# Two-layer network behind an attention block: weights converted without GpSimd, a longer lag between the layers, the narrow block last

## The chip, the cores and the metric

The kernel runs on one core of one Trainium2 chip. The metric is device time in microseconds (us). Of the kernel before, three runs took 1065.77, 1066.15 and 1066.64 us; the median is 1066.15 us. Engines are named as the profile names them: PE (TensorE) with PEld (its weight loads), DVE (VectorE), ACT (ScalarE), POOL (GpSimd), SP (the queue that issues the DMAs).

## The reference, cut to what matters

12480 tokens of 128 channels pass an attention block with 32 inducing points, and then two layers of 2048 hidden units each.

```python
h = mab(I, x)            # 32 inducing rows look at all tokens (softmax over 12480)
a = mab(x, h)            # every token looks at the 32 rows
# first layer, float64 weights
g = s * relu(a @ w_in)**2 + b
y = g @ w_out
# second layer, float64 weights
h2 = y @ w2_in
g2 = where(h2 >= 1, h2, where(h2 <= -1, 0, (h2 + 1)**2 / 4))
out = g2 @ w2_out
```

The four weight matrices arrive as float64, two 32-bit words to a number. [...]

## The kernel before

**Blocks and steps.** The tokens are cut into 25 blocks (`NB`): 24 of 512 tokens and one of 192. The narrow one is block 0 (`tokens`, L86). The 2048 hidden units of a layer are 16 chunks of 128; a step takes two chunks of one block, so a block has 8 steps (`SPB`) and a layer 200. In step t the first layer works on its step t (`in1`, relu, square, split, `out1`) and the second layer on step t minus `LAG` (`in2`, clip, square, `g2`, split, `out2`). `LAG` is 13. A matmul with float32 operands is issued in one piece, and split products (an fp32r high part and an fp32r rest) take three matmuls in place of one.

**Three parts of the program.** In the ramp, a planner (class `Plan`, L102) gives every operation an engine and a start from fixed costs and dependencies, and emits all operations in the order of their planned starts; `JOBS` (L67) is the order in which it is asked. The ramp holds the pass over x (loads, transposes, scores, running maximum and sum, weighted sums) that ends with `hT`, the transposed attention rows; the conversion of the weights; the product of `hT` with `w_in` (`h_w`), which replaces the first matmul of the layer's own weights; and the first 13 steps of the first layer, whose `out1_whole` (L697) multiplies in float32, since the split weights aren't there yet. Then a plain loop (L1025) issues step after step in the order of `ORDER` (L72). The last steps are planned again, in the order of `TJOBS` (L78).

**Conversion.** The weights are 16 pieces of 128x512 numbers (`pieces`, four each of `w_in`, `w_out`, and then `w2_in` and `w2_out` in turn). `convert` (L398) squares the upper word on ACT (L409), makes a mask from it on DVE (L423), shifts and joins the exponent and mantissa bits on DVE (L426, L430), masks the power of two on DVE (L434), scales the lower word on POOL (L415), multiplies (L437) and adds (L442) on POOL. For the second layer's weights a high part (L444) and a rest (L447) follow, the rest by a subtraction in DVE or POOL (L449). `split_out` (L470) does the same for half of `w_out`.

**PSUM.** The tag `h1` has one buffer of two banks, `h2` has two; the ramp's products `pw`, the scores of the first groups and the steps' `in1` take them in turn, and `took` (L826) gives the planner the release that an operation has to wait for. `y1` and `y2` have one bank each.

Of the kernel before, what the change touches and what calls it, by code (L numbers as in the profile page):

```python
# [34 lines left out]
LAG = 13  # L35
# [25 lines left out]
ENG = {"mask": ("DVE",), "sq": ("ACT", "Pool"), "lo": ("Pool",), "mul": ("Pool",), "add": ("Pool",),  # L61
       "hi": ("ACT", "Pool", "DVE"), "rest": ("DVE", "Pool")}
# [39 lines left out]
class Plan:  # L102
# [3 lines left out]
    HOP = 0.2  # L106
    SAME = {"DVE": 0.13, "ACT": 0.15}
# [4 lines left out]
    def find(self, eng, dur, deps, at):  # L112
        t = at
        for d in deps:
            if d is not None:
                t = max(t, d[1] + (self.SAME.get(eng, 0.0) if eng == d[2] else self.HOP))
        line = self.lines.setdefault(eng, [])
        for i, (a, b) in enumerate(line):
            if b <= t:
                continue  # L120
            if a - t >= dur:
                return t, i
            t = max(t, b)
# [1024 lines left out]
```

## Time and profile before

| | |
|---|---|
| median of three runs | 1066.15 us |
| the profiled execution | 1066.77 us, its span 1065.0 us |
| PE busy | 1020.1 us, 96% of the span |
| DVE busy | 834.6 us, 78% |
| ACT busy | 769.1 us, 72% |
| POOL busy | 667.9 us, 63% |
| chain that ended last | PE 88%, DVE 7% |
| mean granted PE clock | 0.977 of full speed |

The table is an average over parts that have different limits. The page's 40 slices show this: PE reads 9 tenths or more from the sixth slice to the last but one, and 7, 7, 7, 4, 8 in the first five, in which the clock row reads 7 to 9 tenths too. The rows below therefore go by stage: up to `hT`, from `hT` to the second layer's first matmul, the settling of both layers, the long even part, and the end.

### The profile page before, as it was taken

What the parts mean: (1) busy time and instruction counts of PE and PEld (TensorE: products, weight loads), DVE (VectorE), ACT (ScalarE), POOL (GpSimd) and SP (SyncE); (2) the same over time, 40 slices, a digit from 0 to 9 for tenths busy, and PEclk for the clock granted to TensorE, in tenths of its full rate; (3) what the DMA queues carried; (4) which work ended last, traced back from release to release, by engine and by line L of the source; (5) the groups of instructions that cost most, each with busy time, mean ns of one, the idle gap of its engine ahead of it and who ended that gap; (6) DMA issues with size and microseconds to landing.
All of it is one profiled execution on the core that took longest, in us unless ns stands there. A gap on an engine that the chain in (4) does not pass through costs nothing.

```text
span 1065.0 us, 11873 instructions
## 1 busy us (share of the span) xinstructions
PE 1020.1 (96%) x4285; PEld 748.9 (70%) x4285; DVE 834.6 (78%) x821; ACT 769.1 (72%) x807; POOL 667.9 (63%) x656
## 2 busy tenths in 40 slices
PE   7774899999999999999999999999999999999997
PEld 5553577777777777777777777777777777777775
DVE  5889768777788777788778788777788778777775
ACT  5425477777777777777777777777777777777754
POOL 3666776656657656567566567565675665656565
PEclk9777899999999999999999999999999999999999
DMA  8522001100001000001000002000011000000001
GB/s 282 198 60 59 1 4 30 20 11 1 11 11 39 10 11 1 11 10 40 10 10 11 1 11 50 0 11 10 1 24 37 0 10 10 1 10 10 10 1 20
DMA packets 65466, 28.25 MB, mean 27 GB/s; under 512 B 54016, under 2 KB 58240, under 8 KB 65408
## 3 DMA queue, kind: packets, MB, share of 16 engines
q1 hardware_dynamic: 65408, 27.49, 10.6%
q8 instruction: 34, 0.56, 0.2%
q14 instruction: 24, 0.20, 0.1%
HBM read 14.80 MB, written 6.39 MB: 20 GB/s over the span
## 4 chain that ended last, share of the span: by engine, by line
PE 88%; DVE 7%; ACT 1%; issue 1%; POOL 1%; DVEq 0%; ACTq 0%; POOLq 0%
PE y L692 15%; PE y L679 9%; PE y L678 8%; PE y L680 8%; PE h L729 8%; PE h L728 8%; PE h L727 8%; PE h L637 8%; PE y L695 4%; PE y L694 4%; PE y L693 4%; DVE g L655 1%; DVE cva_out L426 1%; PE s L572 0%; DVE cva_out L430 0%
## 5 line engine op out<-in xcount | busy, mean ns | idle before, releaser
L734 DVE TENSOR_SCALAR cl<-h 128x1024 f32<-128x1024 f32 (+2 forms) x202 | 238.7, 1184 | 121.0 <-PE h L729 121.0
L201 POOL TENSOR_SCALAR hi<-g 128x512 fp32r<-128x512 f32 x187 | 131.5, 703 | 309.6 <-PE y L695 306.3
L648 ACT ACTIVATE g<-h 128x1024 f32<-128x1024 f32 (+1 forms) x200 | 200.8, 1004 | 158.3 <-PE h L637 155.9
L756 DVE TENSOR_TENSOR lo<-oo,hi 128x1024 fp32r<-128x1024 f32 (+1 forms) x188 | 238.4, 1268 | 69.1 <-ACT hi L197 54.8
L738 ACT ACTIVATE cl<-cl,mhalf 128x1024 f32<-128x1024 f32 (+2 forms) x202 | 226.0, 1121 | 67.5 <-DVE cl L734 67.5
L663 POOL TENSOR_TENSOR lo<-g,hi 128x512 fp32r<-128x512 f32 x187 | 242.3, 1296 | 15.6
L743 DVE SCALAR_TENSOR_TENSOR oo<-h,cl 128x1024 f32<-128x1024 f32 (+2 forms) x202 | 237.2, 1176 | 8.6 <-ACT cl L738 5.1
L653 ACT ACTIVATE g<-g 128x1024 f32<-128x1024 f32 (+1 forms) x195 | 205.0, 1051 | 5.4
L692 PE MATMUL y<-g,wo_w 128*128 128x512 f32 x374 | 191.0, 591 | 0.0
L727 PE MATMUL h<-y1h,wi_hi 128*128 128x512 f32 (+1 forms) x400 | 155.8, 389 | 3.3 <-DVE oo L743 3.3
L678 PE MATMUL y<-hi,wo_hi 128*128 128x512 f32 (+1 forms) x400 | 157.5, 394 | 0.6 <-ACT hi L197 0.6
L729 PE MATMUL h<-y1l,wi_hi 128*128 128x512 f32 (+1 forms) x400 | 156.7, 392 | 0.0
L680 PE MATMUL y<-hi,wo_lo 128*128 128x512 f32 (+1 forms) x400 | 156.7, 392 | 0.0
L728 PE MATMUL h<-y1h,wi_lo 128*128 128x512 f32 (+1 forms) x400 | 156.0, 390 | 0.0
L679 PE MATMUL y<-lo,wo_hi 128*128 128x512 f32 (+1 forms) x386 | 152.6, 395 | 0.9 <-DVE lo L756 0.8
L693 PE MATMUL y<-hi,wo_hi 128*128 128x512 f32 x187 | 148.3, 793 | 0.0
L637 PE MATMUL h<-qt,hw 128*128 128x512 f32 (+1 forms) x400 | 126.3, 399 | 2.4 <-ACT g L648 1.3
L197 ACT CAST hi<-oo 128x1024 fp32r<-128x1024 f32 (+2 forms) x106 | 105.2, 996 | 3.7 <-PE y L680 1.9
L201 POOL TENSOR_SCALAR hi<-oo 128x1024 fp32r<-128x1024 f32 (+1 forms) x96 | 99.3, 1034 | 0.5 <-DVE oo L743 0.5
L678 PEld LDWEIGHTS y<-hi,wo_hi 128*128 128x128 f32 x400 | 75.5, 189 | 22.7 <-POOL lo L663 4.2
L637 PEld LDWEIGHTS h<-qt,hw 128*128 128x128 f32 x400 | 74.6, 189 | 23.6 <-ACT g L648 3.3
L727 PEld LDWEIGHTS h<-y1h,wi_hi 128*128 128x128 f32 x400 | 75.4, 188 | 21.1 <-issue 2.1
(148 smaller groups left out, 1188.6 us busy)
## 6 DMA issues: line engine op xcount, KB each, us to landing
xc<-in_x_dram SPq DMA_DIRECT2D x24, 256.0 KB, 5.6
qin<-se SPq DMA_DIRECT2D x96, 64.0 KB, 2.0
out_dram<-o SPq DMA_DIRECT2D x96, 64.0 KB, 2.2
raw_in<-in_moe_w_in_dram SPq DMA_DIRECT2D x8, 512.0 KB, 5.3
raw_out<-in_moe_w_out_dram SPq DMA_DIRECT2D x8, 512.0 KB, 5.1
xc<-in_x_dram SPq DMA_DIRECT2D x1, 96.0 KB, 1.9
out_dram<-o SPq DMA_DIRECT2D x4, 24.0 KB, 2.7
ind_sb<-in_inducing_dram SPq DMA_DIRECT2D x1, 16.0 KB, 5.1
```

The costliest lines, as they stand in the source:

```text
L637: nc.tensor.matmul(p[:, j, :tb(bl)], hw[f // 4][:, (f % 4) * 128:(f % 4 + 1) * 128], qt[bl], start=True, stop=True)
L663: engine[eng].tensor_sub(lo1[t], g1[t][:, 1:], hi1[t].bitcast(F32))
L678: nc.tensor.matmul(p, whi[:, f, :], hi[:, j, :], start=first, stop=False)
L679: nc.tensor.matmul(p, whi[:, f, :], lo[:, j, :], start=False, stop=False)
L680: nc.tensor.matmul(p, wlo[:, f, :], hi[:, j, :], start=False, stop=last)
L692: nc.tensor.matmul(p, wo_w[:, f0, :], g[:, 0, :], start=(f0 == 0), stop=False)
L727: nc.tensor.matmul(p[:, j, :tb(bl)], wi2_hi[:, fs], y1h[bl], start=True, stop=False)
L728: nc.tensor.matmul(p[:, j, :tb(bl)], wi2_lo[:, fs], y1h[bl], start=False, stop=False)
L729: nc.tensor.matmul(p[:, j, :tb(bl)], wi2_hi[:, fs], y1l[bl], start=False, stop=True)
L734: nc.vector.tensor_scalar(cl[t][:, part(js)], h2[t][:, part(js), :tb(t // SPB)], -1.0, 1.0, op0=ALU.max, op1=ALU.min)
L743: nc.vector.scalar_tensor_tensor(oo[t][:, part(js)], h2[t][:, part(js), :tb(t // SPB)], -1.0, cl[t][:, part(js)], op0=ALU.max, op1=ALU.add)
L756: engine[eng].tensor_sub(lo2[t][:, part(js)], oo[t][:, part(js)], hi2[t][:, part(js)].bitcast(F32))
```

## The change

**Conversion.** ACT takes the absolute value of the upper word, DVE raises it to a smallest value and shifts it (two one-operand operations in place), joins sign and exponent (`c_a`), masks the power of two (`c_p`) and does scaling and multiplication of the lower word in one two-operand operation (`c_mul`). For `w_in` and `w_out` a sum on DVE or POOL follows (`c_add`). For the second layer's weights there is no sum on DVE or POOL: the high part is a copy of the upper sum `cva` on ACT or DVE, and the rest is made on PE, which adds `cva`, minus the high part and the lower word through three matmuls with identity matrices into a PSUM bank of the tag `h2`; ACT or DVE copies the bank out (`c_lo`).

**Plan.** The planner's costs are new, and it has a line "port": an operation on POOL or one on DVE that is marked `DVE+` takes the port for its whole length, so that it never plans the two side by side. Waits for a PSUM buffer also keep the order in which the buffers are taken (`took`). Squares and relus of the ramp's steps may go to ACT or DVE.

**Lag and blocks.** `LAG` is 18, so the ramp holds 18 steps of the first layer, and the last 18 steps hold the second layer alone. The narrow block is block 24, the last; the ramp's steps are all 512 wide. `JOBS` puts weight pieces ahead of x. `YB` is 3. The last steps' jobs are written by `last_jobs`, with every high part on ACT and every rest on POOL.

```diff
-LAG = 13
+LAG = 18
-YB = 2
+YB = 3
-ENG = {"mask": ("DVE",), "sq": ("ACT", "Pool"), "lo": ("Pool",), "mul": ("Pool",), "add": ("Pool",),
-       "hi": ("ACT", "Pool", "DVE"), "rest": ("DVE", "Pool")}
+TS, TT = 0.42, 0.69
+ENG = {"add": (("DVE+", TT), ("Pool", 1.27)), "hi": (("ACT", 0.59), ("DVE+", TS)), "rest": (("DVE+", TT), ("Pool", 1.27)),
+       "lo": (("ACT", 0.59), ("DVE", 0.65))}
...
-x0 c0 i t0 x1 c1 it x2 c2 t1 s0 w0 s1 c3 x3 x4 t2 s2 t3 c4 w1 s3 w2 t4 c5 s4 x5 c6 t5 x6 w3 t6 w4 s5
+c0 i c1 it x0 c2 t0 s0 c3 x1 x2 t1 t2 s1 c4 w0 x3 s2 x4 t3 w1 x5 w2 x6 s3 t4 w3 b4 t5 s4 w4 s5 t6 s6 w5 f z h0 h1 c5
...
 def tokens(bl):
-    if bl:
-        return TP, KB, TB, TB0 + (bl - 1) * TB
-    return TP0, KB0, TB0, 0
+    if bl < NB - 1:
+        return TP, KB, TB, bl * TB
+    return TPL, KBL, TBL, bl * TB
...
     def find(self, eng, dur, deps, at):
+        name = eng.rstrip("+")
+        lines = [self.lines.setdefault(k, []) for k in [name] + (["port"] if eng in ("DVE+", "Pool") else [])]
...
-        def c_t1():
-            nc.vector.scalar_tensor_tensor(new("cva", U32), T["raw", n][:, :, 1], 3, T["cvs", n].bitcast(U32),
-                                           op0=ALU.logical_shift_left, op1=ALU.bitwise_and)
+        def c_abs():
+            nc.scalar.activation(new("cvs", F32), T["raw", n][:, :, 1].bitcast(F32), AF.Abs)
+        def c_top():
+            nc.vector.tensor_scalar_max(T["cvs", n], T["cvs", n], TINY)
+        def c_shift():
+            v = T["cvs", n].bitcast(U32)
+            nc.vector.tensor_scalar(v, v, 3, 0x3FFFFFF8, op0=ALU.logical_shift_left, op1=ALU.bitwise_and)
...
-        def c_mul(eng):
-            engine[eng].tensor_mul(T["cvl", n], T["cvl", n], T["cvs", n])
+        def c_mul():
+            nc.vector.scalar_tensor_tensor(new("cvl", F32 if name in ("in", "out") else F32R), T["raw", n][:, :, 0], 2.0 ** -52, T["cvs", n],
+                                           op0=ALU.mult, op1=ALU.mult)
...
-        def c_rest(eng):
-            hi, lo = (w[:, sl] for w in wparts[name])
-            engine[eng].tensor_sub(lo, T["w", n], hi.bitcast(F32))
+        def c_sum():
+            ps = T["cw", n] = mbank(f"cw{n}")[:, 0, :]
+            nc.tensor.matmul(ps, ident, T["cva", n].bitcast(F32), start=True, stop=False)
+            nc.tensor.matmul(ps, minus_r, wparts[name][0][:, sl], start=False, stop=False)
+            nc.tensor.matmul(ps, ident_r, T["cvl", n], start=False, stop=True)
+        def c_lo(eng):
+            copy(eng, wparts[name][1][:, sl], T.pop(("cw", n)))
...
-        p = mbank(f"h1_{t}") if t < LAG and t % 3 else bank(f"h1_{t}")
+        p = mbank(f"h1_{t}") if t < LAG and t % 2 else bank(f"h1_{t}")
...
-TH = "APPAAAAAAAPAA"
-TL = "PPPPPPPPPDPPD"
+TH = "A"
+TL = "P"
```

**How it moves instructions: one weight piece.** On DVE before, the second piece (`cvs_in_236`, `cva_in_250`) is four instructions, and the pass over x follows:

```order
L423 TENSOR_SCALAR cvs_in_236<-cvs_in_236 128x512
L426 SCALAR_TENSOR_TENSOR cva_in_250<-raw_in_193,cvs_in_236 128x512
L430 SCALAR_TENSOR_TENSOR cva_in_250<-raw_in_193,cva_in_250 128x512
L434 TENSOR_SCALAR cvs_in_236<-cva_in_250 128x512
L293 TENSOR_REDUCE mx_293<-psc_230 128x1
L296 TENSOR_TENSOR m_292<-mx_293,m_202 128x1
L298 TENSOR_SCALAR nm_296<-m_292 128x1
L346 COPY hsum<-ph_275 128x128
```

On POOL before, the same piece (`cvl_in_238`) and the loads of the next two:

```order
L415 TENSOR_SCALAR cvl_in_238<-raw_in_193 128x512
L437 TENSOR_TENSOR cvl_in_238<-cvl_in_238,cvs_in_236 128x512
L442 TENSOR_TENSOR win<-cvl_in_238,cva_in_250 128x512
L415 TENSOR_SCALAR cvl_in_321<-raw_in_243 128x512
L415 TENSOR_SCALAR cvl_in_331<-raw_in_266 128x512
```

On DVE now, the second piece is `cvs_in_164`, `cva_in_183`, `cvl_in_199`:

```order
L440 TENSOR_SCALAR cvs_in_164<-cvs_in_164 128x512
L444 TENSOR_SCALAR cvs_in_164<-cvs_in_164 128x512
L447 SCALAR_TENSOR_TENSOR cva_in_183<-raw_in_147,cvs_in_164 128x512
L451 TENSOR_SCALAR cvs_in_164<-cva_in_183 128x512
L454 SCALAR_TENSOR_TENSOR cvl_in_199<-raw_in_147,cvs_in_164 128x512
L460 TENSOR_TENSOR win<-cvl_in_199,cva_in_183 128x512
L509 COPY iT<-pi 128x32
```

Six instructions stand on DVE where four stood, and the three on POOL are gone.

**The second layer's beginning.** On PE before, behind the first layer's step 12 (`g_12` is its squared product, `y_1` its output) and one more `in1`, the second layer begins with `h_0`, 192 columns wide:

```order
L702 MATMUL y_1_1013<-g_10_1024,wo_w 128x512
L702 MATMUL y_1_1013<-g_10_1024,wo_s 128x512
L702 MATMUL y_1_1013<-g_11_1042,wo_w 128x512
L702 MATMUL y_1_1013<-g_11_1042,wo_s 128x512
L702 MATMUL y_1_1013<-g_12_1055,wo_w 128x512
L702 MATMUL y_1_1013<-g_12_1055,wo_s 128x512
L637 MATMUL h_13_1077<-qt_976,hw_827 128x512
L637 MATMUL h_13_1077<-qt_976,hw_907 128x512
L727 MATMUL h_0_1080<-y1h_1037,wi_hi 128x192
L728 MATMUL h_0_1080<-y1h_1037,wi_lo 128x192
```

On PE now, the last `in1` of this stretch, the float32 products of steps 16 and 17 and the sum of the last weight piece (`cw_1160`) stand ahead of the second layer's `h_0`:

```order
L657 MATMUL h_19_1134<-qt_1023,hw_806 128x512
L657 MATMUL h_19_1134<-qt_1023,hw_829 128x512
L726 MATMUL y_2_1142<-g_16_1088,wo_w 128x512
L726 MATMUL y_2_1142<-g_16_1088,wo_s 128x512
L726 MATMUL y_2_1142<-g_17_1125,wo_w 128x512
L726 MATMUL y_2_1142<-g_17_1125,wo_s 128x512
L468 MATMUL cw_1160<-cva_out_1149,ident 128x512
L469 MATMUL cw_1160<-wo_hi,minus_r 128x512
L470 MATMUL cw_1160<-cvl_out_1155,ident_r 128x512
L751 MATMUL h_0_1167<-y1h_991,wi_hi 128x512
L752 MATMUL h_0_1167<-y1h_991,wi_lo 128x512
L753 MATMUL h_0_1167<-y1l_998,wi_hi 128x512
```

The second layer's first matmul has moved from behind step 13's `in1` to behind step 19's, the float32 products reach to step 17 (`g_17`) and not to step 12, a sum of three matmuls stands ahead, and `h_0` is 512 wide.

**The end.** On PE before, the second layer's last `in2` (`h_199`) stands behind the `out2` of step 195 (`hi_195`; its rest lies in a buffer named `g_195`), 512 wide:

```order
L678 MATMUL y_24_8623<-hi_195_8638,wo_hi 128x512
L679 MATMUL y_24_8623<-g_195_8652,wo_hi 128x512
L680 MATMUL y_24_8623<-hi_195_8638,wo_lo 128x512
L727 MATMUL h_199_8677<-y1h_8452,wi_hi 128x512
L728 MATMUL h_199_8677<-y1h_8452,wi_lo 128x512
L729 MATMUL h_199_8677<-y1l_8461,wi_hi 128x512
```

On PE now, the `in2` of step 198 (`h_198`) stands behind the `out2` of step 192 (`hi_192`, `lo_192`):

```order
L702 MATMUL y_24_8627<-hi_192_8574,wo_hi 128x192
L703 MATMUL y_24_8627<-lo_192_8598,wo_hi 128x192
L704 MATMUL y_24_8627<-hi_192_8574,wo_lo 128x192
L751 MATMUL h_198_8640<-y1h_8333,wi_hi 128x192
L752 MATMUL h_198_8640<-y1h_8333,wi_lo 128x192
L753 MATMUL h_198_8640<-y1l_8335,wi_hi 128x192
```

The last eight steps, 192 to 199, are 192 wide and not 512, and `in2` runs six steps ahead of `out2` there, not four.

## Rows read from the trace of the kernel before

**Rows 1.** Windows by stage: length; busy PE, PEld, DVE, ACT, POOL (count); clock; DMA; GB/s

```profile
0.00:62.85 62.85, 49.28 (x420) 35.75 (x420) 43.15 (x86) 29.85 (x64) 33.32 (x39) 0.82 0.62 211
62.85:116.25 53.40, 34.93 (x122) 21.86 (x121) 50.98 (x67) 20.44 (x32) 38.35 (x32) 0.80 0.18 50
116.25:163.44 47.19, 43.94 (x213) 32.85 (x212) 32.21 (x45) 38.03 (x44) 33.71 (x34) 0.96 0.02 3
163.44:1006.98 843.54, 843.54 (x3340) 621.90 (x3339) 667.40 (x586) 650.69 (x635) 525.78 (x530) 1.00 0.07 13
1006.98:1059.20 52.22, 48.43 (x198) 36.52 (x196) 40.15 (x40) 30.13 (x33) 36.70 (x22) 1.00 0.07 11
1059.20:1065.00 5.80, 0.00 (x0) 0.00 (x0) 0.72 (x1) 0.00 (x0) 0.00 (x0) 0.93 0.30 45
```

**Rows 2.** Timeline of DVE: the first conversion; hT. Start, length, engine, line, operation, [idle before]

```profile
8.72 0.43 DVE L423 TENSOR_SCALAR cvs_in<-cvs_in 128x512 f32<-128x512 f32 x1 [6.47 <-ACT cvs_in L409]
...
62.56 0.29 DVE L546 COPY hT<-pht 128x128 f32<-128x128 f32 x1 [0.41 <-PE pht L521]
```

**Rows 3.** Timeline of PE: the longest wait; the second layer begins

```profile
90.29 5.07 PE L702 MATMUL y<-g,wo_s 128*128 128x192 f32 x16 [6.65 <-DVE g L655]
...
116.25 0.25 PE L727 MATMUL h<-y1h,wi_hi 128*128 128x192 f32 x1
```

**Rows 4.** Timeline of PE, one full step

```profile
163.44 0.63 PE L637 MATMUL h<-qt,hw 128*128 128x512 f32 x2
...
163.91 0.39 PE L727 MATMUL h<-y1h,wi_hi 128*128 128x512 f32 x1
...
165.30 0.40 PE L678 MATMUL y<-hi,wo_hi 128*128 128x512 f32 x1
...
166.71 1.02 PE L692 MATMUL y<-g,wo_w 128*128 128x512 f32 x2
...
168.26 0.63 PE L637 MATMUL h<-qt,hw 128*128 128x512 f32 x2
```

**Rows 5.** Timeline of PE, a narrow step of the second layer

```profile
139.31 0.25 PE L727 MATMUL h<-y1h,wi_hi 128*128 128x192 f32 x1
...
139.96 0.27 PE L678 MATMUL y<-hi,wo_hi 128*128 128x192 f32 x1
```

**Rows 6.** Timeline of PE near the end: a wait for VectorE

```profile
1033.60 0.47 PE L727 MATMUL h<-y1h,wi_hi 128*128 128x512 f32 x1 [1.73 <-DVE oo L743]
```

**Rows 7.** Timeline of DVE near the end: 1024 columns, both operands in SBUF

```profile
1052.28 1.23 DVE L756 TENSOR_TENSOR lo<-oo,hi 128x1024 fp32r<-128x1024 f32 x1 [0.19 <-ACT hi L197]
```

**Rows 8.** Windows of DVE before hT: lines L423, L426, L430, L434, L199 in turn

```profile
0.00:62.85 62.85, 8.23 (x10) 0.82 0.62 211
...
0.00:62.85 62.85, 8.45 (x9) 0.82 0.62 211
...
0.00:62.85 62.85, 7.88 (x9) 0.82 0.62 211
...
0.00:62.85 62.85, 3.48 (x9) 0.82 0.62 211
...
0.00:62.85 62.85, 0.40 (x1) 0.82 0.62 211
```

**Rows 9.** Timeline of DVE, one piece alone, then one beside GpSimd

```profile
17.01 0.43 DVE L423 TENSOR_SCALAR cvs_in<-cvs_in 128x512 f32<-128x512 f32 x1 [4.78 <-ACT cvs_in L409]
17.47 0.69 DVE L426 SCALAR_TENSOR_TENSOR cva_in<-raw_in,cvs_in 128x512 uint32<-128x512 uint32 x1
18.19 0.69 DVE L430 SCALAR_TENSOR_TENSOR cva_in<-raw_in,cva_in 128x512 uint32<-128x512 uint32 x1
...
38.22 1.66 DVE L426 SCALAR_TENSOR_TENSOR cva_out<-raw_out,cvs_out 128x512 uint32<-128x512 uint32 x1
```

**Rows 10.** Timeline of POOL at the same place

```profile
37.98 1.35 POOL L442 TENSOR_TENSOR wo_w<-cvl_out,cva_out 128x512 f32<-128x512 f32 x1
```

**Rows 11.** Window in which PE waited

```profile
85.00:90.00 5.00, 0.00 (x0) 0.00 (x0) 4.93 (x5) 1.12 (x2) 4.37 (x3) 0.50 0.42 103
```

More of the change, by code (lines that the diff above doesn't have):

```diff
@@ L1 @@
+import bisect
 import math
@@ L102 @@
 class Plan:
-    HOP = 0.2
-    SAME = {"DVE": 0.13, "ACT": 0.15}
+    HOP = {"PE": 0.25}
+    SAME = {"DVE": 0.04, "ACT": 0.05, "Pool": 0.05}
     def __init__(self):
@@ L192, in moe_attn_kernel, with took @@
     add, best = plan.add, plan.best
+    left = {"h1": [None], "h2": [None, None]}
+    last = {"h1": 0.0, "h2": 0.0}
+    def took(tag, dur, fn, *deps):
+        op = add("PE", dur, fn, *deps, left[tag][-1 if tag == "h1" else -2], at=last[tag])
+        last[tag] = op[0]
+        return op
     engine = {"ACT": nc.scalar, "DVE": nc.vector, "Pool": nc.gpsimd}
@@ L444, in c_hi @@
         def c_hi(eng):
-            copy(eng, wparts[name][0][:, sl], T["w", n])
-        def c_rest(eng):
-            hi, lo = (w[:, sl] for w in wparts[name])
-            engine[eng].tensor_sub(lo, T["w", n], hi.bitcast(F32))
-        free = P.get(("c_end", n - CVB))
-        raw = P["raw", n]
-        cost = {"mask": {"DVE": 0.34}, "sq": {"ACT": 0.52, "Pool": 1.45}, "lo": {"ACT": 0.52, "Pool": 0.59}, "mul": {"Pool": 1.23, "DVE": 0.6},
-                "add": {"Pool": 1.23, "DVE": 0.6}, "hi": {"ACT": 0.52, "Pool": 0.59, "DVE": 0.34},
-                "rest": {"Pool": 1.23, "DVE": 0.6}}
@@ L466, in convert @@
-        if name in wparts and name != "out":
-            hi = best(one_of["hi"], c_hi, ad)
-            P["c_end", n] = best(one_of["rest"], c_rest, hi)
+            copy(eng, wparts[name][0][:, sl], T["cva", n].bitcast(F32))
+        def c_sum():
[3 more added lines that the diff above has]
+            nc.tensor.matmul(ps, ident_r, T["cvl", n], start=False, stop=True)
@@ new lines, in c_lo @@
+        def c_lo(eng):
+            copy(eng, wparts[name][1][:, sl], T.pop(("cw", n)))
+        t = add("ACT", 0.68, c_abs, P["raw", n], P.get(("c_end", n - CVB)), at=at)
+        t = add("DVE+", TS, c_top, t)
+        t = add("DVE+", TS, c_shift, t)
+        a = P["c_a", n] = add("DVE+", TT, c_a, t)
+        t = add("DVE+", TS, c_p, a)
+        t = P["c_mul", n] = add("DVE+", TT, c_mul, t)
+        if name in ("in", "out"):
+            P["c_add", n] = P["c_end", n] = best(ENG["add"], c_add, t, bias=CB)
+        else:
+            hi = best(ENG["hi"], c_hi, a)
+            t = took("h2", 1.33, c_sum, hi, t, P["hT"])
+            P["c_end", n] = best(ENG["lo"], c_lo, t)
+            left["h2"].append(P["c_end", n])
@@ L958, in plan_step @@
         if name == "in1":
-            stage(name, u, "PE", 0.41, in1, p("qt", bl), free("relu1", u, 1, "h1"), p("in1", u - 1))
+            stage(name, u, "PE", pe(GW, bl), in1, p("qt", bl), free("relu1", u, 1, "h1"), p("in1", u - 1))
         elif name == "relu1":
@@ L975, in plan_step @@
         elif name == "in2":
-            stage(name, u, "PE", 1.22, in2, p("y1", bl), wchunk("in2", u), free("g2", u, 2, "h2"), p("in2", u - 1))
+            stage(name, u, "PE", pe(6, bl), in2, p("y1", bl), wchunk("in2", u), free("g2", u, 2, "h2"), p("in2", u - 1))
         elif name == "clip2":
@@ L988, in plan_step @@
         elif name == "out2":
-            stage(name, u, "PE", 1.22, out2, p("lo2", u), wchunk("out2", u), p("out2", u - 1), p("store", u // SPB - 1))
+            stage(name, u, "PE", pe(6, bl), out2, p("lo2", u), wchunk("out2", u), p("out2", u - 1), p("store", u // SPB - 1))
     def both_steps(t):
```

256 lines of the change are left out of this document (124 added, 132 removed).

## The prediction

> **What bounds the kernel now.** I read the windows by stage first, then the chain of waits on the page, then the timelines of PE and DVE. The windows cut the run into five parts [rows 1]. From 163.44 to 1006.98 us PE is busy for all of 843.54 us at clock 1.00, with DVE at 79% and ACT at 77%: there PE alone sets the time, and only PE work taken out of this part, or moved ahead of it, is worth anything. From hT (62.85 us, [rows 2]) to the second layer's first matmul (116.25 us, [rows 3]) PE is busy for 34.93 of 53.40 us at a mean clock of 0.80, and DVE for 50.98: there DVE binds. Up to hT neither is full (PE 49.28, DVE 43.15 of 62.85). So the ramp, which DVE paces, has free PE time, and the even part has none.
>
> A full step is in1 0.47, in2 1.39, out2 1.41, out1 1.55 us, 4.82 in all [rows 4]. A fp32r matmul of 512 columns takes 0.47/2 = 0.235 there, so the float32 one in out1 takes 1.55 - 3 x 0.23 = 0.86. A narrow step's in2 takes 0.65 [rows 5]; I take 0.66 for its out2, and 0.87 for its in1 and out1 together (five matmuls at 0.11, and 0.86 x 192/512 = 0.32).
>
> **PE work behind the second layer's first matmul (call its start S).** Before, S is 116.25, and steps 14 to 199 of in1 and 13 to 199 of out1 are still to come, with the whole second layer: 186 x 0.47 + 187 x 1.55 + 192 x 2.80 + 8 x 1.31 + 24 blocks' scores at 0.25 = 87.4 + 289.9 + 537.6 + 10.5 + 6.0 = 931.4 us. (The 0.25: the even part's 843.54 us are 174 steps at 4.82, 838.7, and five groups of four blocks' scores, so 0.97 a group.) The rest of the span is 1065.0 - 116.25 = 948.8, so 17.4 us are no matmul at full clock: 5.8 behind the last one [rows 1], about 5 of waits among the last steps (the longest 1.73, [rows 6]), and 6.4 while the layers settle up to 163.44.
>
> Now, step 19's in1 and step 17's out1 stand ahead of S. Left are 172 full in1 (80.8), 174 full out1 (269.7), 8 narrow steps of the first layer (7.0), the second layer as before (537.6 + 10.5) and 20 blocks' scores (5.0): 910.6. That is 20.8 less. Two edits share it: five steps of lag, and a narrow block that no longer uses up eight of the ramp's steps. Waits behind S: 5.5 behind the last matmul (transpose and store are narrower, the DMA's own delay stays), 5.5 at the end, and 3 while the layers settle, since in2 of step 2 must wait for the clip chain of step 0: 14.0. The bounds of this term are 9 and 20: at the lower end no settling and little waiting among narrow steps, at the upper end POOL, which now makes every rest, and DVE, which has 1.23 us for a full-width two-operand operation [rows 7] and three such each step, pace the eight mixed steps and the last ten full ones. So the span is S + 910.6 + 14.0 = S + 924.6.
>
> **S, first part: hT.** The five conversion lines take 8.23 + 8.45 + 7.88 + 3.48 + 0.40 = 28.4 us of DVE before hT [rows 8], so the pass over x takes 43.15 - 28.4 = 14.7. A piece alone shows what an operation costs from start to start: 0.46 with one tensor operand, 0.72 with two [rows 9]. Beside POOL it costs more: the one at 38.22 takes 1.66 instead of 0.69, while POOL's sum holds from 37.98 to 39.33 [rows 9, 10]. Now six pieces with six operations each (3 x 0.46 + 3 x 0.72 = 3.54) are 21.2, two with five are 5.6, and two operations of the ninth 0.9: 27.7. DVE therefore works 42.4 us before hT, as before; the change is that it may wait less. Before, it waited 19.7 us: 6.47 of it for the first piece, which came behind four loads of x [rows 2], and more for later pieces, which ran behind x too. Now the pieces' loads go ahead of x. I take a start at 5.5 (no sooner than 5, no later than the 8.72 of before) and 5 of waits in the last chain of small operations through PE, ACT and DVE: hT at 53. Its bounds are 48 and 63, the latter if x, now behind 0.5 to 1 MB of weights, ends the pass as late as before.
>
> **S, second part: from hT to S.** On DVE stand: the rest of eight pieces, 8 x 2.82 - 0.9 = 21.7; 16 squares 1024 wide, by the nearest row 1.23 and a gap, 1.26 each [rows 7] = 20.2; four products with the attention rows, 2.9; the softmax of the first block and of the first group, an estimated 6.8 (six full-width operations at 0.72 and small ones); three turns, two rests and one copy at 0.72, 4.3. Sum 55.9. This is more than the 50.98 of before, with five more steps done in it. Waits: 5 in the first 8 us, where the first softmax goes back and forth between PE, DVE and ACT; 3 for relus later; 2 for the few operations left on POOL, which can each cost a DVE operation about 1 us. So 66 us, and S = 53 + 66 = 119. Bounds are 57 (nearly no waits) and 80 (below). ACT was busy for 20.44 of 53.40 there [rows 1]; even twice that fits into 66. PE has in the same 66 us: 20 in1 (9.4), 18 out1 in float32 at 2 x 0.86 (31.0), eight sums at 0.86 + 0.47 (10.6), four products (3.4), scores and small ones (1.8): 56.2 at full clock. It fits, but with 10 us to spare, and this is the step I trust least.
>
> **Sum.** 119 + 924.6 = 1043.6 us of span. The profiled execution's time was 1066.77 with a span of 1065.0, 1.8 more, and the median of the runs is 0.6 below that execution, so 1043.6 + 1.2 = **1044.8 us**, against 1066.15.
>
> **Where a page and the rows are weighed.** In the window from 85 to 90 us PE has no work and its clock reads 0.50, the lower level of 1.2 GHz [rows 11]; its wait there lasts 6.65 us [rows 3]. In the even part the clock is 1.00 [rows 1]. The Trainium skill ("TensorE: Matmul & The Clock Gate", part 1) says that the lower clock is the state at rest and that sustained work releases the upper one. By that rule, and the trace agrees, a ramp in which PE works for 56 of 66 us would run mostly at the upper level, and the sum above stands; a ramp with holes in it would not, and that is the second and the last case below.
>
> **The rivals.**
> (a) *PE becomes the bound of the ramp.* If the clock between hT and S stays at the mean of before, 0.80 [rows 1], PE needs 56.2 / 0.80 = 70 us, and starts in earnest some 8 us behind hT: S = 53 + 78 = 131, and the time 1056.8. For it: PE was half idle there and cold for parts of it. Against it: PE is handed twice the work, and the planner fills the holes ahead of the first out1 with idle matmuls. Chance 0.15.
> (b) *hT isn't earlier.* The pass over x may be held by x and not by DVE, whose work is the same 42 us. Then S = 63 + 66 = 129, and 1054.8. For it: the loads of x now come later. Against it: DVE was busy for nearly all of the stretch in which most of x is worked on, and its conversions were drawn out by POOL. Chance 0.12.
> (c) *DVE hardly waits.* hT at 50 and 57 us from there give S = 107, and 1032.8. For it: POOL has next to nothing left in the ramp. Against it: operations on three engines hang on each other in every step. Chance 0.12.
> (d) *Slower.* The same place as (a), with the clock down: the change trades DVE and POOL work for float32 matmuls, and the span grows as soon as S passes 1065.0 - 924.6 = 140.4, which is PE's 56.2 us in 140.4 - 53 - 8 = 79.4, a mean clock of 0.71. At 0.60 PE needs 94 us, S = 155, and the time is 1080.8. For it: the clock was 0.50 in the window behind a long wait. Against it: it needs waits through the whole ramp, and the sums of the second layer's pieces are spread over it. Chance 0.05.
>
> **How the numbers follow.** The forecast with S between 114 and 125 (1039.8 to 1050.8) has 0.54, the cases (a) to (d) 0.15, 0.12, 0.12 and 0.05, and a gain that is given back in full 0.02. About 0.2% is what a measurement of this kernel can tell from no change, some 2 us. Faster by more than that: 0.54 + 0.15 + 0.12 + 0.12 = 0.93; within it 0.02; slower 0.05. The range takes in (a), (b) and (c) and the bounds of the waits: 1032 to 1060.
>
> **What would show it.** The step rows of the even part should read 4.82 us again, with PE full: then the 20.8 us stand. hT should be copied near 53, the second layer's in2 of step 0 should start near 119, and DVE should be busy for over 80% between the two, with conversions at 0.43 and 0.69 and few drawn out. If PE is full and its clock below 0.9 there, (a) was right; if hT is at 60 or later with DVE idle before it, (b). A step of 4.95 us in the even part, or more than 20 us of waits behind S, would make the forecast wrong from a side that I gave no case of its own.

## The result, and the profile after

The changed kernel takes 1049.19 us (median of four runs, 1047.86 to 1051.75), the kernel before 1065.96 (four runs); the ratio is 0.9846, 95% interval 0.9825 to 0.9867. The forecast was 1044.8 with a range of 1032 to 1060. The profiled execution took 1049.8 us, its span is 1047.9.

The windows of the changed kernel by stage, with the columns of [rows 1]: up to hT, from hT to the second layer's first matmul (S), the settling, the long even part, the end, and what follows the last matmul.

```profile
0.00:52.83 52.83, 38.84 (x426) 27.87 (x426) 38.81 (x100) 31.43 (x67) 6.08 (x14) 0.99 0.75 252
52.83:120.90 68.07, 65.06 (x197) 33.90 (x198) 53.36 (x80) 39.04 (x52) 6.32 (x8) 0.96 0.14 39
120.90:163.50 42.60, 41.52 (x168) 29.74 (x167) 34.35 (x29) 31.62 (x32) 26.68 (x26) 1.00 0.00 1
163.50:990.00 826.50, 825.67 (x3289) 609.58 (x3288) 679.51 (x585) 635.16 (x626) 534.20 (x525) 1.00 0.08 14
990.00:1042.00 52.00, 48.50 (x257) 39.91 (x255) 40.59 (x48) 34.31 (x46) 37.24 (x28) 1.00 0.07 11
1042.00:1047.90 5.90, 0.39 (x2) 0.22 (x2) 0.38 (x1) 0.00 (x0) 0.00 (x0) 0.78 0.12 17
```

Against [rows 1] the three parts are: up to hT 62.85 and now 52.83 (-10.0), from hT to S 53.40 and now 68.07 (+14.7), behind S 948.75 and now 927.0 (-21.75); the sum is -17.1, the difference of the two spans. The second line is the one to look at. PE was busy for 34.93 of 53.40 us at clock 0.80, and is now busy for 65.06 of 68.07 at 0.96. GpSimd, 38.35 us there before, has 6.32.

The marks of the forecast stand as follows. On DVE, the first conversion and hT, which answer to [rows 2]:

```profile
5.49 0.43 DVE L440 TENSOR_SCALAR cvs_in<-cvs_in 128x512 f32<-128x512 f32 x1 [2.42 <-ACT cvs_in L436]
...
52.54 0.29 DVE L565 COPY hT<-pht 128x128 f32<-128x128 f32 x1 [0.41 <-PE pht L540]
```

On PE, the longest wait between hT and S, and S itself, which answer to [rows 3]; then the first layer's product in two steps of the even part, which answers to [rows 4]:

```profile
91.34 1.12 PE L726 MATMUL y<-g,wo_w 128*128 128x512 f32 x2 [1.22 <-DVE g L679]
...
120.90 0.40 PE L751 MATMUL h<-y1h,wi_hi 128*128 128x512 f32 x1
...
149.08 1.02 PE L716 MATMUL y<-g,wo_w 128*128 128x512 f32 x2
...
153.90 1.02 PE L716 MATMUL y<-g,wo_w 128*128 128x512 f32 x2
```

The wait of 6.65 us is gone, the longest is 1.22. A full step is 153.90 - 149.08 = 4.82 us, as before.

### The profile page after: what moved, and what is told of

Same layout as the page of the kernel before. It is cut to its first block, busy times and chain, and to the rows that moved or that the text cites. A ratio compares the mean times of both kernels' runs of the same rounds, so it can differ in the third digit from the quotient of the medians.

```text
span 1047.9 us, 11983 instructions
## 1 busy us (share of the span) xinstructions
PE 1020.0 (97%) x4332; PEld 741.2 (71%) x4332; DVE 847.0 (81%) x841; ACT 771.6 (74%) x822; POOL 610.5 (58%) x597
## 4 chain that ended last, share of the span: by engine, by line
PE 87%; DVE 5%; POOL 3%; issue 2%; ACT 2%; DMA 1%; SPq 0%; POOLq 0%; DVEq 0%; ACTq 0%
PE y L716 14%; PE y L703 8%; PE y L702 8%; PE y L704 8%; PE h L657 8%; PE h L753 8%; PE h L751 8%; PE h L752 8%; PE y L718 4%; PE y L717 4%; PE y L719 4%; PE y L726 2%; DVE lo L780 1%; DMA xc<-in_x_dram 1%; DVE g L679 1%
## 5 line engine op out<-in xcount | busy, mean ns | idle before, releaser
L780 DVE TENSOR_TENSOR lo<-oo,hi 128x1024 fp32r<-128x1024 f32 x182 | 258.1, 1418 | 44.2 <-ACT hi L226 23.1
L230 POOL TENSOR_SCALAR hi<-g 128x512 fp32r<-128x512 f32 (+1 forms) x182 | 126.6, 695 | 277.8 <-PE y L719 252.4
L687 POOL TENSOR_TENSOR lo<-g,hi 128x512 fp32r<-128x512 f32 (+1 forms) x182 | 233.3, 1282 | 15.2
L677 ACT ACTIVATE g<-g 128x1024 f32<-128x1024 f32 (+1 forms) x184 | 191.0, 1038 | 5.0
L716 PE MATMUL y<-g,wo_w 128*128 128x512 f32 (+1 forms) x364 | 181.3, 579 | 0.0
L702 PE MATMUL y<-hi,wo_hi 128*128 128x512 f32 (+1 forms) x400 | 157.5, 394 | 0.0
L753 PE MATMUL h<-y1l,wi_hi 128*128 128x512 f32 (+1 forms) x400 | 156.4, 391 | 0.0
L717 PE MATMUL y<-hi,wo_hi 128*128 128x512 f32 (+1 forms) x182 | 142.1, 781 | 0.0
L657 PE MATMUL h<-qt,hw 128*128 128x512 f32 (+1 forms) x400 | 124.1, 394 | 0.0
L226 ACT CAST hi<-oo 128x1024 fp32r<-128x1024 f32 (+2 forms) x111 | 108.4, 979 | 8.3 <-DVE oo L767 4.5
L230 POOL TENSOR_SCALAR hi<-oo 128x1024 fp32r<-128x1024 f32 x91 | 95.6, 1051 | 14.4 <-DVE oo L767 14.4
```

Of the source, the lines that this page charges most:

```text
L657: nc.tensor.matmul(p[:, j, :tb(bl)], hw[f // 4][:, (f % 4) * 128:(f % 4 + 1) * 128], qt[bl], start=True, stop=True)
L687: engine[eng].tensor_sub(lo1[t], g1[t][:, 1:], hi1[t].bitcast(F32))
L702: nc.tensor.matmul(p, whi[:, f, :], hi[:, j, :], start=first, stop=False)
L716: nc.tensor.matmul(p, wo_w[:, f0, :], g[:, 0, :], start=(f0 == 0), stop=False)
L753: nc.tensor.matmul(p[:, j, :tb(bl)], wi2_hi[:, fs], y1l[bl], start=False, stop=True)
L780: engine[eng].tensor_sub(lo2[t][:, part(js)], oo[t][:, part(js)], hi2[t][:, part(js)].bitcast(F32))
```

## The experiments

The forecast let DVE pace the ramp and gave PE free time there. But PE is nearly full in it. That makes two theories: with P, PE is the bound from hT to the end, and it matters little on which side of S its work stands; with D, DVE paces the ramp, and work moved ahead of S is work saved. In the edits below, `...` stands for lines left out. The table lists all twelve runs. Ratios are to the kernel before; hT, S and the rest of the span are those of the profiled execution.

| run | median | ratio, 95% interval | hT | S | behind S |
|---|---|---|---|---|---|
| changed kernel | 1049.2 | 0.9846 (0.9825-0.9867) | 52.8 | 120.9 | 927.0 |
| e1 LAG 13 | 1045.7 | 0.9805 (0.9789-0.9822) | 52.5 | 110.0 | 933.3 |
| e2 narrow block first | 1050.7 | 0.9852 (0.9822-0.9882) | 51.2 | 102.6 | 940.1 |
| e3 products on GpSimd | 1053.0 | 0.9883 (0.9865-0.9902) | 53.2 | 126.1 | 926.6 |
| e4 sums on VectorE | 1054.0 | 0.9890 (0.9866-0.9914) | 52.3 | 107.6 | 943.5 |
| e5 LAG 13, narrow first | 1051.3 | 0.9866 (0.9850-0.9881) | 51.2 | 107.1 | 942.5 |
| e6 x first | 1055.6 | 0.9901 (0.9886-0.9915) | 54.0 | 124.5 | 929.7 |
| e7 conversion of before | 1064.4 | 0.9994 (0.9980-1.0008) | 53.6 | 108.2 | 959.8 |
| e8 no idle matmuls | 1048.3 | 0.9842 (0.9813-0.9872) | 52.4 | 118.6 | 927.1 |
| e9 no port line | 1052.6 | 0.9878 (0.9866-0.9891) | 53.1 | 121.3 | 928.1 |
| e10 LAG 13, more idle | 1055.0 | 0.9905 (0.9889-0.9920) | 52.5 | 115.6 | 933.4 |
| e11 more idle | 1058.3 | 0.9939 (0.9921-0.9958) | 53.9 | 126.6 | 927.0 |
| e12 LAG 13, no idle | 1045.0 | 0.9802 (0.9789-0.9816) | 51.9 | 107.9 | 933.3 |

One of the four runs of e1 took 4489.71 us; it is left out of the ratio, and the other three took 1043.22 to 1046.28. S is where the second layer's first matmul starts. It isn't the same border in every row: in e2, e4 and e7 the planner puts that matmul ahead of the `out1` of the ramp's last two, two and four steps.

**e1, the lag alone undone.**

```diff
-LAG = 18
+LAG = 13
...
-... a12 q2 a13 c10 c11 c12 c13 a14 a15 c14 a16 a17 c15 q3
+... a12 q2 c10 c11 c12 c13 c14 c15
```

> The changed kernel with LAG 13 and JOBS shortened to 13 steps; all else as it is. In the changed kernel PE is busy for 65.06 of the 68.07 us from hT (52.83) to the second layer's first matmul S (120.90). Theory P (PE is the bound there): five steps fewer stand ahead of S, 5 x (0.47 + 1.72) = 10.95 us of PE, so S falls to about 110 to 112, and 5 x 2.02 = 10.1 us more stand behind it: the time stays within 2 us of 1049.2, 1048 to 1051. Rival D (DVE paces the ramp and its PE time is free, as the prediction reasoned): DVE only loses some squares, S falls by 6 at most, the time is 1053 to 1054 and more. Rival L (the five steps of lag are worth their full 10.1 us): S stays at 121 and the time is 1059.

The window from hT to S of e1:

```profile
52.50:109.96 57.46, 54.11 (x169) 28.62 (x169) 46.48 (x74) 32.97 (x46) 5.02 (x5) 0.95 0.16 46
```

S falls by 10.94 us, as much as the five steps' PE work that P named (10.95), and PE is as full as with the longer lag (54.11 of 57.46). Behind S only 6.3 us come back and not 10.1, so the time falls by some 4 us. P is right on S and on the direction, but the time lies 2 us below its 1048 to 1051. D (S down by 6 at most, 1053 and more) and L are out. The 3.8 us that didn't come back are waits: behind S the changed kernel has 927.0 - 910.6 = 16.4 us that are no matmul at full clock, e1 by the same count 933.3 - 920.7 = 12.6 (below).

**e2, the block alone undone.**

```diff
-    if bl < NB - 1:
-        return TP, KB, TB, bl * TB
-    return TPL, KBL, TBL, bl * TB
+    if bl:
+        return TP, KB, TB, TBL + (bl - 1) * TB
+    return TPL, KBL, TBL, 0
...
```

> The changed kernel with the narrow block as block 0, as in the kernel before; lag, conversion and JOBS as they are. Theory P (PE is the bound from hT on): eight ramp steps are narrow, some 8 x 1.2 = 9.5 us less PE work ahead of S, S falls to about 112, and 8 x 1.15 = 9.2 more stand behind it: the time stays within 3 us of 1049.2. Rival D (ramp's PE time is free): S moves by under 4 and the time is 1055 to 1058.

S falls by 18.3 us and 13.1 come back behind it (P had counted 9.5 and 9.2) in the profiled execution, which took 1045.07 us; the other three runs took 1050.33 to 1052.94. Much of what goes beyond P's count is no gain: the `out1` of two steps, one `in1` and the sum of one weight piece, 5.2 us of PE work by the forecast's prices, stand behind S here and ahead of it in the changed kernel. What differs between the four runs is the mean clock: 0.998 in the first, 0.992 to 0.994 in the others. The medians are 1.5 us apart, the intervals overlap: P's figure, not D's 1055 to 1058.

**e5, both undone.** The edits of e1 and e2 together.

> The changed kernel with LAG 13 and the narrow block first, as both were in the kernel before; conversion, plan and order of the loads as changed. Theory P (PE is full from hT on, so where its work stands is worth nothing; the gain is that of conversion and plan alone): the time is within 4 us of the 1045.7 and 1050.7 that the two edits gave one by one, 1043 to 1051. Rival L (one edit stood in for the other; together they carry the 20.8 us): 1058 to 1066.

The windows of e5, from hT to S and behind S:

```profile
51.16:107.14 55.98, 46.52 (x160) 27.88 (x161) 40.21 (x75) 28.72 (x46) 7.70 (x9) 0.91 0.16 48
107.14:1049.60 942.46, 932.79 (x3744) 688.75 (x3742) 736.10 (x663) 717.57 (x710) 597.12 (x581) 1.00 0.07 13
```

Behind S are 15.5 us more than in the changed kernel, and S is 13.8 earlier: lag and block together are worth 2 us of the 16.8, with intervals that overlap. Rival L is out, but P isn't the whole account either: PE isn't full in this ramp, it has 9.5 us of holes (46.52 of 55.98) where the changed kernel has 3.0, and 1051.3 is at the end of what P allowed. By the forecast's count the two edits together put 20.8 us of PE work ahead of S. S rose by 13.8, so 7.0 found room in the holes and in a higher clock (0.91 and 0.96). Behind S the waits rose from 942.5 - 931.4 = 11.1 to 16.4 us, and that took 5.3 of it back.

The two edits aren't alike. With LAG 13, the narrow block first (e5) is at 0.9866 and last (e1) at 0.9805: some 6 us, with intervals that don't overlap, where the ramp had holes. From there the longer lag (the changed kernel) loses some 4. With LAG 18 the block's place (e2 against the changed kernel) can't be told from no change.

**e7, the conversion of before.**

```diff
...
-        t = P["c_mul", n] = add("DVE+", TT, c_mul, t)
...
-            t = took("h2", 1.33, c_sum, hi, t, P["hT"])
-            P["c_end", n] = best(ENG["lo"], c_lo, t)
...
+        t0 = add("Pool", 0.59, c_scale, P["raw", n], ...)
+        t = P["c_mul", n] = add("Pool", 1.27, c_prod, t, t0)
+        P["c_add", n] = P["c_end", n] = add("Pool", 1.27, lambda: c_add("Pool"), t)
+        if name not in ("in", "out"):
+            t = add("ACT", 0.59, lambda: copy("ACT", ...), P["c_add", n])
+            P["c_end", n] = best(ENG["rest"], c_rest, t, bias=CB)
```

> The changed kernel with all 16 pieces' scaling, product and sum on GpSimd, and the second layer's rest by a subtraction on VectorE or GpSimd, in place of the sums on TensorE; lag, block and order of loads as changed. GpSimd gets 16 x 3.13 = 50 us of work, VectorE loses 8 x 1.44 and 8 x 0.72 but works beside it, TensorE loses 10.6. Theory G (taking the conversion off GpSimd is what filled the ramp): hT stays near 53, the second layer begins or settles 10 us or more later, and the time is 1059 to 1066. Rival N (the conversion's place is worth little, the order of the loads and the plan carry the gain): 1046 to 1054.

The whole gain is gone: the ratio is 0.9994. The profiled execution is the slowest of the ten, 1069.83 us; the others took 1062.78 to 1065.54. hT stays (the plan has six pieces' sums ahead of it, the changed kernel eight), and S comes early, but the second layer can't go on behind it. The timelines of e7 around that place: PE, then DVE, then GpSimd.

```profile
143.84 0.80 PE L746 MATMUL h<-y1h,wi_hi 128*128 128x512 f32 x1 [19.74 <-DVE oo L762]
```

```profile
125.53 1.17 DVE L470 TENSOR_TENSOR wo_lo<-cvl_out,wo_hi 128x512 fp32r<-128x512 f32 x1 [3.45 <-ACT wo_hi L226]
...
132.76 0.69 DVE L470 TENSOR_TENSOR wi_lo<-cvl_in,wi_hi 128x512 fp32r<-128x512 f32 x1 [3.14 <-ACT wi_hi L226]
...
138.41 1.80 DVE L470 TENSOR_TENSOR wo_lo<-cvl_out,wo_hi 128x512 fp32r<-128x512 f32 x1 [2.82 <-ACT wo_hi L226]
140.13 2.34 DVE L753 TENSOR_SCALAR cl<-h 128x1024 f32<-128x1024 f32 x2
```

```profile
129.43 1.30 POOL L461 TENSOR_TENSOR cvl_in<-cvl_in,cvs_in 128x512 f32<-128x512 f32 x1 [3.28 <-DVE cvs_in L451]
130.82 1.26 POOL L466 TENSOR_TENSOR cvl_in<-cvl_in,cva_in 128x512 f32<-128x512 f32 x1
```

A piece goes from DVE to GpSimd (product, sum), to ACT (high part) and back to DVE (rest), and nobody is full on the way: DVE waits 1.8 to 3.5 us for each of the last five pieces' high part, and GpSimd 2.3 to 4.7 for DVE's. From 107 to 140.1 us DVE is busy for 18.3 of 33.1 us, ACT for 19.2 and GpSimd for 18.2. The second layer's first clip (`cl`, L753) stands behind the last of these rests on DVE: the matmuls it reads ended at 109.88, and it starts at 140.13. PE waits 19.74 us. Of DVE's 13 two-operand operations on 128x512 between 101 and 140 us, 11 take 0.68 or 0.69: in this kernel the round trip through an engine that takes its instructions in order costs, and hardly the drawn-out operations. In the changed kernel DVE hands a piece on once, to PE, and doesn't wait for it.

e7 shows that the gain hangs on the conversion; it doesn't show that the kernel before lost its time in the same way. e7 keeps the planner's line for the port, which plans GpSimd and DVE apart, and the kernel before had no such line. How much of the 15 us is that spacing is open: no run has e7 without the line.

**e3, products and sums of the first layer's pieces on GpSimd.** The same edit for `w_in` and `w_out` alone.

```diff
...
+            t0 = add("Pool", 0.59, c_scale, P["raw", n], ...)
+            t = P["c_mul", n] = add("Pool", 1.27, c_prod, t, t0)
-            P["c_add", n] = P["c_end", n] = best(ENG["add"], c_add, t, bias=CB)
+            P["c_add", n] = P["c_end", n] = add("Pool", 1.27, lambda: c_add("Pool"), t)
```

> The changed kernel with the scaling, the product and the sum of the eight pieces of w_in and w_out on GpSimd, as before; the order of loads, the lag and the block's place stay. Theory G (GpSimd holding the shared port draws DVE's conversions out, which is why taking it away brought hT from 62.85 to 52.83): DVE operations beside POOL take 1.3 to 1.7 us in place of 0.69, hT is at 56 to 61, and the time 1052 to 1058. Rival O (it is the order of the loads that brought hT forward): DVE has 8 x 1.44 us less to do, hT stays within 2 us of 52.83, and the time within 2 us of 1049.2.

Neither theory: hT stays within half a microsecond (O), yet the time is in G's range. Two pieces have moved behind hT, and from there to S it takes 72.84 us in place of 68.07. hT by itself says little, then; it must be read with the number of pieces done by it.

**e6, x ahead of the weights.**

```diff
-c0 i c1 it x0 c2 t0 s0 c3 x1 x2 t1 t2 s1 c4 w0 x3 ...
+x0 c0 i t0 x1 c1 it x2 c2 t1 s0 w0 s1 c3 x3 x4 ...
-XPACE = 0
+XPACE = 4.5
```

> The changed kernel with the loads and jobs of x ahead of the weights again (the order of JOBS of before, x paced at 4.5 us); all else as changed. With the products on GpSimd hT stayed at 53.2, so it isn't GpSimd's port that held hT at 62.85. Theory O (the order of the loads does it, since the last piece before hT comes late and DVE idles first): hT at 57 to 63, the time 1053 to 1059. Rival K (DVE's own work or the planner's order of the pass sets it): hT stays at 51 to 55, the time at 1047 to 1051.

hT is at 54.0 (K), the time 6 us up (O's range): again six pieces are done by hT and not eight, 2.4 us more pass from hT to S and 2.7 more behind it. The pieces from `c5` on keep the changed kernel's places, so this isn't the whole order of before.

**e9, the planner without its line for the port.**

```diff
-... for k in [name] + (["port"] if eng in ("DVE+", "Pool") else [])]
+... for k in [name]]
```

> The changed kernel with the planner's line for the shared port left out: it may plan an operation of GpSimd beside one of VectorE again. Theory Q (with the conversion off GpSimd there is little for the line to keep apart: GpSimd is busy for 12 us up to the second layer's start): the time is within 3 us of 1049.2. Rival R (the line is what keeps VectorE's operations from being drawn out, in the ramp and while the layers settle): S later than 124 and the time 1053 or more.

S hardly moves (121.3). The median is 3.4 us up, just past Q's 3, and the intervals just meet; R's later S didn't come. At the median the line is worth some 3 us; it may be worth nothing.

**e4, the last sums on VectorE.**

```diff
...
-            hi = best(ENG["hi"], c_hi, a)
-            t = took("h2", 1.33, c_sum, hi, t, P["hT"])
-            P["c_end", n] = best(ENG["lo"], c_lo, t)
...
+            t = add("DVE+", TT, c_w, t)
+            t = add("ACT", 0.59, c_whi, t)
+            P["c_end", n] = add("DVE+", TT, c_rest, t)
```

> The changed kernel with the last sum of the second layer's weights on VectorE (a sum and a subtraction at 0.72 each, high part on ACT) in place of three matmuls and a copy. PE loses 8 x 1.33 = 10.6 us ahead of S, DVE gains about 11 and then has 64 of work in 68. Theory P (PE alone is the bound): S falls by 5 to 10, the time is 1040 to 1045. Rival D (DVE paces): S rises by 8 to 11, the time is 1057 to 1060. If both are near their limit, S moves by under 5 and the time stays at 1047 to 1054.

S falls by 13.3, more than P's 5 to 10: the last pieces' operations and the `out1` of two steps now come behind it, and there DVE is late. The window behind S, and the largest wait of PE in this kernel (total, times, longest):

```profile
107.64:150.00 42.36, 31.80 (x112) 20.46 (x111) 35.50 (x44) 28.12 (x30) 16.01 (x16) 0.88 0.00 0
```

```profile
PE h L750 <- DVE oo L766: 10.0, 2, 8.4
```

None of the three expectations came: P's S with a time 9 us above P's 1040 to 1045, and the time that was expected if both engines are near their limit (1047 to 1054), but not its S. PE was handed 10.6 us less ahead of S and nothing was gained by it, so PE alone isn't the bound: with 11 us more DVE becomes one.

**e8, e10, e11 and e12, the idle matmuls and the clock.** e8 leaves them out; e10 (LAG 13) and e11 make them finer and put six into the hole in front of the first scores; e12 is e1 without them.

```diff
-    for t in plan.gaps("PE", P["ex", NG - 2][1], P["hT"][0], cost, IDLE):
-        add("PE", cost, on_idle0, P["ex", NG - 2], at=t)
-    for t in plan.gaps("PE", P["hT"][1], P["out1", 0][0], cost, IDLE):
-        add("PE", cost, on_idle, P["hT"], at=t)
```

```diff
-IW = 128
-IDLE = 0.05
+IW = 64
+IDLE = 0.0
...
+    t = P["pht"][1]
+    while t + cost <= P["st"][0]:
+        add("PE", cost, on_idle0, P["ex", NG - 2], at=t)
+        t += cost
```

> The changed kernel without the idle matmuls that the planner puts into TensorE's holes ahead of hT and of the first out1. They take 4.0 us of TensorE behind hT, beside real work that waits. Theory W (they keep the granted clock up): without them the clock reads 0.5 to 0.8 for longer than the 8 us behind hT in the changed kernel, S is 2 to 6 us later, the time is 1051 to 1056. Rival F (they only fill holes that are waits for VectorE): S within 1 us of 120.9, the time 1047 to 1050.

> The changed kernel with LAG 13, idle matmuls of 64 columns without a margin, and six of them in the hole between the product that gives hT and the first softmax's scores. In the runs so far the granted clock fell to 0.50 at hT for some 6 us in most profiles, and in one (narrow block first) it stayed at 1.00: span 1042.7 there, 1048.0 to 1050.6 in the other runs of that kernel, at clocks of 0.992 to 0.994. Theory W (a fuller TensorE around hT keeps the clock up): mean clock 0.998 and over, the time 1040 to 1043. Rival F (it doesn't reach what the clock goes by, or the idle matmuls cost what they give): 1044 to 1047, as with LAG 13 alone.

> The same idle matmuls in the changed kernel with its LAG of 18. Theory W: mean clock 0.998 and over, the time 1043 to 1046. Rival F: 1047 to 1051. Between this run and the one with LAG 13 the lag is compared a second time: theory P (TensorE is full from hT on) says a smaller lag is 0 to 4 us faster in both.

> The changed kernel with LAG 13 and without idle matmuls, the two edits that were faster or equal one by one (1045.7 and 1048.3, against 1049.2). Theory P (TensorE is full from hT on, so each of its instructions that isn't needed is a loss): 1042 to 1046. Rival W (without them the clock stays low for longer, and the ramp of 13 steps has less to cover it with): 1047 and more. The more idle matmuls of the two runs before gave 1055 and 1058, so at least the direction is with P.

Without them nothing is lost (e8, F's time; S came 2.3 us earlier, where F had 1 and W a later one). With more of them the time rises by 9 us at either lag, against both theories: e11's windows show the clock down at hT all the same.

```profile
53.93:57.00 3.07, 3.07 (x16) 3.07 (x16) 0.59 (x1) 0.62 (x1) 0.00 (x0) 0.50 0.00 0
57.00:61.00 4.00, 4.00 (x13) 2.95 (x13) 2.92 (x11) 0.90 (x2) 0.00 (x0) 0.50 0.00 0
61.00:65.00 4.00, 4.00 (x29) 3.26 (x28) 0.59 (x1) 0.59 (x1) 0.00 (x0) 0.90 0.00 0
```

The added matmuls take longer than planned (16 of them, from 62.06 us on, take 3.68 us, 0.23 apiece, where the planner has 64/595 = 0.11) and stand ahead of the real ones; S is 5.7 us later than in the changed kernel and in e1, and the rest of the span is the same (927.0 and 933.4). The profiled executions are the fastest of e10 and e11; why the medians rose by 9 and not by 5.7 stays open. LAG 13 is again the faster, by 3.2 us. e12, with LAG 13 and no idle matmuls, came as P had it (1042 to 1046) at 0.9802: with e1 (0.9805) the fastest version tried, ahead of the changed kernel by intervals that don't overlap.

## Why the prediction was right, point by point

**The sum.** 53 + 66 + 924.6 = 1043.6 us of span were forecast, 52.8 + 68.1 + 927.0 = 1047.9 came: the terms were off by -0.2, +2.1 and +2.4.

**Up to hT.** The first piece was started at 5.49 (forecast 5.5), and a piece alone takes 0.43 and 0.69, as in [rows 9]. DVE worked 38.8 us, not 42.4 (conversions 26.3 where the forecast had 27.7, the pass over x 12.5 where it had 14.7), and waited 14.0, not 10.6: two misses that cancel. Of the 10 us by which this part is shorter, 4.3 are less work of DVE and 5.7 less waiting. Which edit gave them isn't shown: with the conversion or the order of the loads put back (e3, e6, e7) the plan moves two pieces behind hT, and hT stays.

**The 20.8 us.** As a count they are right: 21.75 us went from behind S, 20.8 of work and 1.0 of waits. As a reason they are wrong, and this is the step that failed: "the ramp, which DVE paces, has free PE time". It had it before [rows 1]. In the changed kernel PE is busy for 65.06 of 68.07 us: of the 10 us that the forecast had PE "to spare", 3.0 are left. DVE is busy for 78%, not over 80. Undone alone or together, lag and block change the time by -4 to +2 us (e1, e2, e5); with the shorter lag the ramp had holes that the block could fill, and for the longer lag few were left (e1: 3.4 us). The chain that ended last says the same of the two kernels. Followed back from S to hT, 44.7 of its 53.4 us before were operations of DVE and 4.6 of PE; now 40.7 of 68.1 are PE's, and 19.0 DVE's, most of them behind 91 us. The forecast came out by luck in this term: 66 us were worked out for DVE, and that was also about what PE needed, 56.2 of work at a mean clock of 0.96, 4.0 of idle matmuls and 3.0 of waits, 65.5 in all.

**Where the gain is.** e7 takes all of it back with the conversion alone; e3 and e4, which each put back a part of it, cost 4 and 5 us. In the kernel before DVE was hardly waiting between hT and S (50.98 of 53.40 us busy). Its operations took longer there, beside GpSimd's 38.35 us. The second layer's pieces on DVE between hT and S, two lines of before and then the two that answer to them (count, busy us, mean ns):

```profile
L426 DVE SCALAR_TENSOR_TENSOR cva_out<-raw_out,cvs_out 128x512 uint32<-128x512 uint32 x4 | 4.7, 1163 | 0.1
L434 DVE TENSOR_SCALAR cvs_out<-cva_out 128x512 uint32<-128x512 uint32 x4 | 3.6, 898 | 0.1
...
L447 DVE SCALAR_TENSOR_TENSOR cva_out<-raw_out,cvs_out 128x512 uint32<-128x512 uint32 x4 | 2.7, 679 | 0.1
L451 DVE TENSOR_SCALAR cvs_out<-cva_out 128x512 uint32<-128x512 uint32 x4 | 2.0, 502 | 0.1
```

The 28 operations of the four conversion lines (L423, L426, L430, L434) took 24.3 us there, where 0.69 and 0.43 apiece [rows 9] make 15.7. Now 38 such operations take 21.6, where the same prices make 20.5. With that the chain left DVE, PE's holes in the ramp closed, and the clock was up: 34.93 of 53.40 us busy at 0.80 became 65.06 of 68.07 at 0.96. That the one follows from the other is read from the traces; no run separates it. The order of the loads carries some 6 us of the gain (e6), the port's line at most a few (e9). The runs were made one edit at a time, and the shares don't add up to 16.8.

**Behind S.** 16.4 us are no matmul at full clock; 14.0 were forecast. 2.0 of the excess are three steps of the even part with 5.45 to 5.51 us in place of 4.82, a cost that the forecast didn't have. PE waits there for a rest on DVE. The timelines of the first of them, PE, DVE and GpSimd:

```profile
784.65 0.50 PE L703 MATMUL y<-lo,wo_hi 128*128 128x512 f32 x1 [0.40 <-DVE lo L780]
```

```profile
781.29 3.31 DVE L780 TENSOR_TENSOR lo<-oo,hi 128x1024 fp32r<-128x1024 f32 x1 [0.82 <-POOL hi L230]
```

```profile
781.22 1.04 POOL L621 TENSOR_TENSOR se<-se,mx 96x512 f32<-96x512 f32 x1
782.23 1.28 POOL L738 TENSOR_TENSOR y1l<-y1f,y1h 128x512 fp32r<-128x512 f32 x1
783.49 1.58 POOL L230 TENSOR_SCALAR hi<-g 128x512 fp32r<-128x512 f32 x1
```

The rest takes 3.31 us, where [rows 7] has 1.23. Its end at 784.60 fits a start of the work when GpSimd's two operations are over, at 783.5, and GpSimd's next one then takes 1.58 in place of its usual 0.70. The Trainium skill ("SBUF — State Buffer", section "SBUF: two separate sides") says that a VectorE operation with two inputs in SBUF and a GpSimd operation hold a shared pair of ports in turn, the later one blocked for the whole of the other; the rows agree. Over the even part the same line has a mean of 1.42 us with LAG 18 and 1.31 with LAG 13 (e1). That the lag shifts the two layers' work on the two engines against each other would explain it, but isn't shown. e1 has 0.9 us of such steps. The rest of its 3.8 us less is in the tail (from the last `in1` to the last matmul 36.7 us, 4.5 of them waits by the steps' prices, against 52.5 with 6.3: 1.8), the settling and the end.

**The clock.** From hT to S it averaged 0.96, down for the first 6 us and then at 1.00. The Trainium skill ("TensorE: Matmul & The Clock Gate", part 1) says that sustained work releases the upper level; for the ramp as a whole the rows agree. Why it is down at its beginning no run here settles (last section). The forecast's "second and the last case" are its rivals (a) and (d).

**The rivals.** (a) named the right mechanism for most of the ramp, a full PE, with too low a clock (0.80 and not 0.96). (b), (c) and (d) did not come about.

## What to carry to other kernels

Work moved out of a full stretch into one with holes is a gain only while the holes last: count the engine's work on both sides of the border after the change, and if it is full on both, the border's place is worth nothing. Of two such moves, count the second with the holes that the first has left: here the block's move was worth some 6 us and the longer lag behind it cost some 4. When one engine's chain of small operations is shortened, ask which engine is the next to be full, and size the sum by that one. A round trip through another engine, in a queue that takes its instructions in order, can hold up all that stands behind it: in e7 some 50 us of GpSimd work (16 pieces at the planner's 3.13) cost 15 us of the whole time, with GpSimd itself never full.

## What the runs showed of the hardware that was not expected

The granted clock at hT is not the same in executions of like programs. In the changed kernel it is down for 6 us from hT on:

```profile
52.83:56.83 4.00, 3.95 (x12) 2.91 (x13) 2.35 (x8) 1.00 (x3) 0.00 (x0) 0.50 0.00 0
56.83:60.83 4.00, 4.00 (x23) 2.97 (x22) 1.75 (x5) 1.10 (x2) 0.00 (x0) 0.75 0.01 4
60.83:64.83 4.00, 4.00 (x22) 1.71 (x20) 3.27 (x6) 1.71 (x3) 0.00 (x0) 1.00 0.00 0
```

In e2's profiled execution it stayed up:

```profile
51.21:57.00 5.79, 5.74 (x35) 4.30 (x36) 4.81 (x15) 2.06 (x5) 0.00 (x0) 1.00 0.01 3
57.00:61.00 4.00, 3.67 (x23) 1.97 (x22) 3.46 (x7) 2.90 (x7) 0.00 (x0) 1.00 0.00 0
```

That execution was 5 to 8 us faster than the three others of its kernel. In the last stretch before hT the two look alike but for the clock, first the changed kernel and then e2:

```profile
50.00:52.83 2.83, 2.32 (x16) 1.78 (x14) 2.35 (x9) 0.88 (x2) 1.27 (x1) 0.86 0.03 13
...
49.00:51.21 2.21, 1.70 (x13) 1.35 (x12) 1.90 (x8) 0.41 (x1) 1.19 (x1) 1.00 0.00 0
```

In the 6 us before these windows PE is busy for 6.00 in both (matmuls of one column among others). So PE's busy time before hT doesn't tell these two executions apart, and filling the holes with 64-column matmuls did not hold the clock in e11.
